# The tiles that TensorE reads in the feed-forward products at the lowest SBUF addresses: one core, local attention and a softplus feed-forward

## The chip, the core and the metric

The program runs on one core of a Trainium2 chip. The metric is the device time of one execution in microseconds (us), taken as the median of several runs. One execution was also recorded by the hardware profiler. Engines are named as in its page: PE is TensorE's matmul side, PEld its weight loads, DVE is VectorE, ACT ScalarE, POOL GpSimd, SP the engine that issues the DMAs.

## What is computed

Long-short attention (a window of 16 positions to each side, and one summary key and value for each block of 32), then a feed-forward network with softplus between its two products. Cut to what matters:

```python
k_sum = k.reshape(B, H, nb, 32, D).max(axis=3)      # B, H, S, D = 4, 8, 768, 64
v_sum = v.reshape(B, H, nb, 32, D).mean(axis=3)
scores_l = where(abs(i - j) < 16, q @ k.T / 8, -1e9)
scores_s = q @ k_sum.T / 8 + log(32)
a = softmax(concatenate([scores_l, scores_s], -1))
x = (a @ concatenate([v, v_sum], 2)).transpose(0, 2, 1, 3).reshape(3072, 512)
h = x @ w_in                                        # 512 -> 2048
g = maximum(h, 0) + log1p(exp(-abs(h)))             # softplus
out = g @ w_out                                     # 2048 -> 512
```

Everything comes in and leaves as float32.

## The kernel before

**Precision.** Both feed-forward products run in the type fp32r. Each operand is kept as two tiles or two halves of one, a rounded high part and the rest, and a product is made of three matmuls (high x high, high x rest, rest x high: `TERMS`).

**Tokens.** The 3072 tokens are worked on in six groups x = 0 to 5 of 512 (two chunks of 256). For each group the attention is done first (scores `sc`, L642, mask and maximum L655, exponential L663, division L676/L679, transposition, values `xo`, L740).

**Phases of the feed-forward.** `w_in` and `w_out` are cut into 16 pieces f of the hidden size; only 8 lie in SBUF at a time, in eight places of the pool `wts`. The phases run groups 0 to 4 over f = 0 to 7, then group 5 over all 16, then groups 4 down to 0 over f = 8 to 15. In the phases that begin at f = 0, `hidden` (L1058) makes one bank `ph` of 128x512 from 12 matmuls: the stationary operand is a piece of `w`, the moving one 512 columns of `xw`, the split input of the group. In the phases that begin at f = 8, `hidden_pair` (L1098) makes the two banks `hx` and `hy` of a pair of f by a Strassen-Winograd scheme with seven products of six 128x256 matmuls each; the moving operands are seven tiles `x` (operands 0 to 6), the stationary ones `w` or its sums `sw`.

**Second product.** ACT applies the softplus to the bank and writes the high part `gh` (L1160), then once more in place (L1164); DVE writes the rest `gl` (L1168). `feed_forward` (L1175) then adds 12 matmuls to four banks `po`: the stationary operand is a 128-column piece of `gh` (8 of the 12) or `gl` (4), the moving one 512 columns of `w`.

**Order.** What each engine does and in which order is written out by hand: `SEQUENCE` lists the tasks by number, `Order.issue` runs them in that order, and the semaphores between the engines follow from who writes and reads which tile. Nothing chooses an order by cost.

**Where tiles lie.** An SBUF tile has its address from its pool. Pools are laid out one after another in the order in which they are opened (`const`, `wts`, `work`), and within a pool each tag, with its number of buffers, gets its place when it first comes up. `wts` holds the weights `w` and, between them, the four places s0 to s3 of `sw` (and of the keys `kf` and values `st` that the attention sums up); `work` holds everything else, among it the inputs' places x0 to x6, `gh` and `gl`. `xw` of an odd group x uses the places x1 and x2 (two buffers each), `xw` of an even one the places x3 to x6.

Of the kernel before, what the change touches and what calls it, by code (L numbers as in the profile page):

```python
# [10 lines left out]
F32 = mybir.dt.float32  # L11
F32R = mybir.dt.float32r
# [220 lines left out]
def kernel(  # L233
# [11 lines left out]
    P = 128  # L245
    B, NHP, _, S = kT.shape
# [3 lines left out]
    NCC = DM // P  # L250
# [5 lines left out]
    CH = CHUNK  # L256
# [3 lines left out]
    CT = 2 * CH  # L260
# [5 lines left out]
    NU = 4  # L266
    NG = 2
# [4 lines left out]
    order = Order()  # L272
    const = ctx.enter_context(tc.tile_pool(name="const", bufs=1))
    wts = ctx.enter_context(tc.tile_pool(name="wts", bufs=1))
    work = ctx.enter_context(tc.tile_pool(name="work", bufs=2))
    dram = ctx.enter_context(tc.tile_pool(name="dram", bufs=3, space=bass.MemoryType.DRAM))
    psum = ctx.enter_context(tc.tile_pool(name="psum", bufs=2, space=bass.MemoryType.PSUM))

    def buffer(shape, dtype, name, tag=None, bufs=None, pool=work, dynamic=False):
        return Buffer(order, pool, shape, dtype, name, tag, bufs, dynamic)  # L280
# [48 lines left out]
        return buffer([P, 2 * WC], F32, name, tag=f, pool=wts, bufs=1)  # L329

    def sums_of(p, name):
        return buffer([P, 2, NU, CH], F32 if name == "first" else F32R, name, tag=f"s{p}", pool=wts, bufs=1)

    def operands(n, name):
        if n < 3:
            return buffer([P, 2, NG, CH], F32R, name, tag=f"x{n}", bufs=2)
        return buffer([P, 2, NG * CH], F32R, name, tag=f"x{n}", bufs=1)

    def block(n, name="r"):
        return buffer([P, NG * CH], F32, name, tag=f"r{n}")  # L340
# [2 lines left out]
    class Sums:  # L343
# [12 lines left out]
        def declare(self):  # L356
            order.group = f"s{self.b}"
            n_t = BLOCK // NHP
            rows = v_hp[self.b].rearrange("hp (n t) c -> (hp n) t c", t=BLOCK)
            self.kf = [buffer([P, 2, S], F32, "kf", tag=f"s{n}", pool=wts, bufs=1) for n in range(NHP // 2)]  # L360
            self.keys = lambda hp: self.kf[hp // 2]()[:, hp % 2]
            self.key_of = lambda hp: (self.kf[hp // 2], hp % 2)
            for i in range(NHP):
                st = buffer([P, n_t, P], F32, "st", tag=f"s{2 + i % 2}", pool=wts, bufs=1)

                def load_k(i=i):
                    nc.sync.dma_start(out=self.keys(i), in_=kT[self.b, i])
                order.add(SP, 0, load_k, [], [self.key_of(i)], size=384 * KiB, row=3072)

                def max_k(i=i):  # L370
                    self.max_keys(i, 0, self.keys(i))
                order.add(DVE, dve(S), max_k, [self.key_of(i)], [(self.k, i)])

                def load_v(i=i, st=st):
                    nc.sync.dma_start(out=st()[:NR], in_=rows[:, i * n_t:(i + 1) * n_t])
                order.add(SP, 0, load_v, [], [st], size=384 * KiB, row=4096)

                def sum_v(engine, st=st, i=i):
                    rows, v = st()[:NR], self.v()
                    for n in (4, 2):  # L380
                        engine.tensor_tensor(rows[:, :n], rows[:, :n], rows[:, n:2 * n], op=ALU.add)
                    if i:
                        engine.tensor_tensor(rows[:, 0], rows[:, 0], rows[:, 1], op=ALU.add)
                        engine.tensor_tensor(v, v, rows[:, 0], op=ALU.add)
                    else:
                        engine.tensor_tensor(v, rows[:, 0], rows[:, 1], op=ALU.add)
                order.add(
                    POOL, 3.0, lambda f=sum_v: f(nc.gpsimd), [st], [self.v],
                    ways=[Way(DVE, 1.8, lambda f=sum_v: f(nc.vector), port=True)],
                )  # L390

            def mean():
                nc.vector.tensor_scalar_mul(self.v(), self.v(), 1.0 / BLOCK)
            order.add(DVE, 0.22, mean, [], [self.v], port=True)
# [1 line left out]


        def declare_first(self):
            self.kf = [buffer([P, S], F32, "kf0", tag=f"x{1 - hp // 2}", bufs=2) for hp in range(NHP)]
            self.keys = lambda hp: self.kf[hp]()  # L400
            self.key_of = lambda hp: self.kf[hp]

            def load_k(hp):
                nc.sync.dma_start(out=self.keys(hp), in_=kT[self.b, hp])

            def max_k(hp):
                self.max_keys(hp, 0, self.keys(hp))
            for hp in range(NHP):
                order.add(SP, 0, lambda hp=hp: load_k(hp), [], [self.kf[hp]], size=384 * KiB, row=3072)
                order.add(DVE, dve(S), lambda hp=hp: max_k(hp), [self.kf[hp]], [(self.k, hp)])  # L410
# [39 lines left out]
    x_bufs = {}  # L450
# [148 lines left out]
    def whole_x(x):  # L599


        if x not in x_bufs and not x % 2:
            x_bufs[x] = [(buffer([P, 1, 2, CT], F32R, "xw", tag=f"x{3 + cc}", bufs=1), 0) for cc in range(NCC)]
        elif x not in x_bufs:
            x_bufs[x] = [(buffer([P, 1, 2, CT], F32R, "xw", tag=f"x{1 + cc % 2}", bufs=2), 0) for cc in range(NCC)]
        return x_bufs[x]

    def kept(x, n):
# [264 lines left out]
    def temporary(pair, outer, which, n):  # L873


        places = {
            (1, 0): ("x2", work, 2), (2, 0): ("x2", work, 2),
            (4, 0): ("q" if not which else "v", work, 1), (4, 1): ("k" if not which else "sp", work, 1),
            (5, 0): ("tb", work, 1), (5, 1): ("pT", work, 1), (6, 0): ("v", work, 1), (6, 1): ("sp", work, 1),
            (7, 0): ("tb", work, 1), (7, 1): ("pT", work, 1),  # L880
        }
        if (pair, outer) not in places:
            return buffer([P, n], U32, "t", "t", T_BUFS, dynamic=True)
        tag, pool, bufs = places[pair, outer]
        return buffer([P, n], U32, "t", tag, bufs, pool)
# [249 lines left out]
    def feed_forward(x, f0, f1):  # L1135
        po = [buffer([P, DM], F32, "po", "po", NT, psum) for _ in range(NT)]
        pairs = f0 > 0
        for f in range(f0, f1):
            if f0 == 0 and f == HALF:
                arrive(range(HALF, NF))  # L1140
            order.group = f"f{x}.{f}"
            if not pairs:
                hs, n = hidden(x, f), 0
            elif f % 2 == 0:
                hs, n = hidden_pair(x, f), 0
            else:
                n = 1
            order.group = f"f{x}.{f}"
            h = hs[n]
            halves = [(h, 0), (h, 1)] if pairs else [h]  # L1150
            w2, i2, _ = w_out_of[f]
            gh = buffer([P, CT], F32R, "gh", bufs=4)
            gl = buffer([P, CT], F32R, "gl", bufs=4)

            def all_of(h=h):
                return h().rearrange("p n c -> p (n c)") if pairs else h()


            def rounded(gh=gh, all_of=all_of):
                nc.scalar.activation(gh(), all_of(), AF.Softplus)  # L1160
            order.add(ACT, act(CT, True), rounded, halves, [gh], table="softplus")

            def exact(all_of=all_of):
                nc.scalar.activation(all_of(), all_of(), AF.Softplus)  # L1164
            order.add(ACT, act(CT, True), exact, [], halves, table="softplus")

            def rest(gh=gh, gl=gl, all_of=all_of):
                nc.vector.tensor_sub(out=gl(), in0=all_of(), in1=gh().bitcast(F32))  # L1168
            order.add(DVE, dve(CT), rest, [*halves, gh], [gl])

            def project(tokens, which, f=f, w2=w2, i2=i2, gh=gh, gl=gl):
                for t in tokens:
                    for i, (a, part) in enumerate(((gh, 0), (gh, 1), (gl, 0))):
                        if (a is gl) in which:
                            nc.tensor.matmul(  # L1175
                                po[t](), lhsT=a()[:, t * P:(t + 1) * P], rhs=w2()[:, part, i2 * DM:(i2 + 1) * DM],
                                start=f == f0 and i == 0, stop=f == f1 - 1 and i == 2,
                            )
            parts = [(w2, i) for i in range(2)]
            if f in (f0, f1 - 1):  # L1180
                for t in range(NT):
                    order.add(
                        PE, 0.7, lambda t=t, p=project: p([t], (False, True)), [gh, gl, *parts], [po[t]],
                    )
            else:
                every = range(NT)
                order.add(PE, 0.47 * NT, lambda p=project: p(every, (False,)), [gh, *parts], po)
                order.add(PE, 0.235 * NT, lambda p=project: p(every, (True,)), [gl, *parts], po)
# [45 lines left out]
    sums = Sums(0)  # L1234
# [67 lines left out]
    for x, f0, f1 in phases:  # L1302
        if x and not f0:
            sums = attend(x, sums)
# [43 lines left out]
```

## Time and profile before

| | us |
|---|---|
| median of 3 runs | 628.8 (627.85 to 631.18) |
| the profiled execution: its own time | 628.08 |
| the profiled execution: span from first to last instruction | 626.3 |
| PE busy in the span | 605.3 (97%) |
| PEld / DVE / ACT / POOL busy | 506.5 / 391.6 / 349.7 / 180.7 |

A matmul's end is modelled in the profile, and it is longer than the distance to the next one's start: consecutive matmuls overlap, and "busy" hides short stops. How fast PE goes is read from how many matmuls a stretch holds: the chain of the work that ended last counts them without overlap, and the timeline gives starts. The granted clock of TensorE is at its full level, 2.4 GHz, from 50 us after the start on.

### The profile page before, as it was taken

The page shows a single profiled execution, that of the slowest core. Times are in us where ns is not written, and L with a number is a line of the kernel's source. Part 1 is how long each engine was busy: PE and PEld are TensorE (multiplying, and loading weights), DVE is VectorE, ACT ScalarE, POOL GpSimd, SP SyncE. Part 2 cuts the span into 40 slices and gives each one's busy share as a digit, 9 for nine tenths or more (in the row PEclk, how much of TensorE's full clock was granted, in tenths as well). Part 3 has the DMA queues.
Part 4 walks back from the last instruction along what each step waited for, and adds up shares of the span by engine and source line. Part 5 has one row for each costly group of instructions (what it writes and reads, how often), then busy time and mean ns, then how long its engine had stood idle before and what let it go on. Part 6 is the DMA issues. An engine that isn't in the chain of part 4 may idle for free.

```text
span 626.3 us, 12000 instructions
## 1 busy us (share of the span) xinstructions
PE 605.3 (97%) x4452; PEld 506.5 (81%) x4452; DVE 391.6 (63%) x1010; ACT 349.7 (56%) x859; POOL 180.7 (29%) x180
## 2 busy tenths in 40 slices
PE   7668999999999999999999999999999999999997
PEld 6457777887787887888888888889888888989895
DVE  5989998686466755444316579873665664564532
ACT  4899999779667676665436886442312322132211
POOL 4444354041314222121000754474410325003000
PEclk9989999999999999999999999999999999999999
DMA  8986777977667676567435640023040230030031
GB/s 295 331 265 188 221 227 232 266 220 247 228 194 253 196 248 210 179 186 239 119 104 178 213 148 1 1 89 113 1 168 2 100 135 1 34 102 1 36 101 67
DMA packets 66570, 96.12 MB, mean 153 GB/s; under 512 B 5872, under 2 KB 44624, under 8 KB 65744
## 3 DMA queue, kind: packets, MB, share of 16 engines
q1 hardware_dynamic: 66512, 95.36, 48.0%
q8 instruction: 35, 0.57, 0.4%
q14 instruction: 23, 0.19, 0.1%
HBM read 66.06 MB, written 27.26 MB: 149 GB/s over the span
## 4 chain that ended last, share of the span: by engine, by line
PE 82%; DVE 6%; DMA 4%; SPq 3%; ACT 3%; issue 1%; ACTq 0%; DVEq 0%
PE po L1175 40%; PE ph L1058 20%; PE hx L1098 9%; PE hy L1098 7%; PE xo L740 3%; PE sc L642 2%; DMA squares<-tb 1%; DVE sp L655 1%; DMA kf<-kT_dram 1%; SPq L721 1%; SPq L513 1%; DVE w L972 1%; SPq L530 1%; ACT sp L679 1%; DVE ks L351 1%
## 5 line engine op out<-in xcount | busy, mean ns | idle before, releaser
L1175 PE MATMUL po<-w,gh 128*128 128x512 f32 x768 | 206.4, 397 | 0.0
L1175 PEld LDWEIGHTS po<-w,gh 128*128 128x128 f32 x768 | 141.6, 188 | 31.7 <-issue 0.6
L1058 PE MATMUL ph<-xw,w 128*128 128x512 f32 x672 | 163.1, 393 | 1.0 <-DVE xw L774 1.0
L1058 PEld LDWEIGHTS ph<-xw,w 128*128 128x128 f32 x672 | 125.7, 188 | 30.0 <-DVE xw L774 1.4
L1175 PE MATMUL po<-w,gl 128*128 128x512 f32 x384 | 116.1, 396 | 0.0
L1175 PEld LDWEIGHTS po<-w,gl 128*128 128x128 f32 x384 | 71.0, 188 | 15.9 <-issue 0.3
L663 ACT ACTIVATE sp<-sp,nm 128x120 f32<-128x120 f32 x192 | 73.1, 385 | 4.9 <-DVE nm L655 4.6
L1160 ACT ACTIVATE gh<-hx 128x512 fp32r<-128x512 f32 x20 | 12.0, 598 | 107.3 <-DVE hx L1108 107.3
L961 POOL TENSOR_TENSOR t<-t,raw 128x1024 int32<-128x1024 int32 (+1 forms) x20 | 41.9, 2100 | 95.8 <-DVE t L947 74.4
L1168 DVE TENSOR_TENSOR gl<-ph,gh 128x512 fp32r<-128x512 f32 x56 | 38.2, 686 | 45.1 <-ACT ph L1164 44.9
L1160 ACT ACTIVATE gh<-ph 128x512 fp32r<-128x512 f32 x56 | 33.4, 597 | 47.4 <-PE ph L1058 47.1
L802 POOL TENSOR_TENSOR x<-r,x 128x512 fp32r<-128x512 f32 x23 | 30.5, 1337 | 68.3 <-DVE x L795 58.6
L655 DVE CUSTOM_DVE_ANT_0 sp<-sc,added 128x120 f32<-128x120 f32 x192 | 40.9, 277 | 4.7 <-PE sc L642 3.9
L663 ACT ACTIVATION_READ_ACCUMULATOR sp<-sp,nm 128x1 f32 x192 | 36.4, 190 | 0.0
L1098 PE MATMUL hx<-x,w 128*128 128x256 f32 x240 | 35.6, 284 | 0.0
L1098 PE MATMUL hx<-x,sw 128*128 128x256 f32 x240 | 35.4, 283 | 0.0
L1098 PEld LDWEIGHTS hx<-x,w 128*128 128x128 f32 x240 | 32.7, 189 | 2.4
L1160 ACT ACT_TABLE_LOAD x23 | 29.5, 1283 | 8.9 <-PE ph L1058 8.6
L1098 PE MATMUL hy<-x,sw 128*128 128x256 f32 x240 | 34.1, 282 | 0.0
L1164 ACT ACTIVATE ph<-ph 128x512 f32<-128x512 f32 x56 | 33.0, 592 | 0.0
L1098 PEld LDWEIGHTS hx<-x,sw 128*128 128x128 f32 x240 | 31.8, 188 | 0.8
L709 DVE STREAM_TRANSPOSE tb<-sp 128x1024 f32<-128x1024 f32 x20 | 24.8, 1240 | 10.4 <-POOL sp L676 5.4
(113 smaller groups left out, 842.4 us busy)
## 6 DMA issues: line engine op xcount, KB each, us to landing
squares<-tb SPq DMA_DIRECT2D x20, 512.0 KB
pT<-squares SPq DMA_DIRECT2D x80, 128.0 KB
raw<-w_out_dram SPq DMA_DIRECT2D x16, 512.0 KB
kf<-kT_dram SPq DMA_DIRECT2D x16, 384.0 KB
raw<-w_in_dram SPq DMA_DIRECT2D x6, 1024.0 KB
q<-qT_dram SPq DMA_DIRECT2D x20, 256.0 KB
raw<-r SPq DMA_DIRECT2D x20, 256.0 KB
part<-ob SPq DMA_DIRECT2D x10, 512.0 KB
```

The lines of the kernel that those rows point to most:

```text
L655: nc.vector.tensor_tensor_reduce(out=sp()[:, n], in0=unit(n), in1=added()[:, kinds.index((lows[w], lows[w + 1]))], scale=-SCALE, scalar=FL ...
L663: nc.scalar.activation(sp()[:, n], sp()[:, n], AF.Exp, bias=nm()[:, n:n + 1], scale=-1.0, accum_out=ss()[:, n:n + 1],)
L709: nc.vector.transpose(out=tb().rearrange("p k (u q) -> p u k q", q=SQ), in_=tiles.sp().rearrange("p u (k q) -> p u k q", q=SQ),)
L740: nc.tensor.matmul(xo()[h * D:(h + 1) * D, g * CH + w * QW:g * CH + (w + 1) * QW], lhsT=tiles.v(g)[:, w, h * D:(h + 1) * D], rhs=queries(g ...
L802: engine.tensor_tensor(to(1), a(), to(0).bitcast(F32), op=ALU.subtract)
L961: nc.gpsimd.tensor_tensor(a, a, word(0, I32), op=ALU.add)
L1058: nc.tensor.matmul(ph(), lhsT=lhs(part, cc), rhs=xw[cc][0]()[:, xw[cc][1], a], start=cc == 0 and n == 0, stop=cc == NCC - 1 and n == 2,)
L1098: nc.tensor.matmul(to()[:, half], lhsT=lhs(wa, cc), rhs=of_x(xa)[:, cc * CH:(cc + 1) * CH], start=cc == 0 and m == 0, stop=cc == NG - 1 an ...
L1160: nc.scalar.activation(gh(), all_of(), AF.Softplus)
L1164: nc.scalar.activation(all_of(), all_of(), AF.Softplus)
L1168: nc.vector.tensor_sub(out=gl(), in0=all_of(), in1=gh().bitcast(F32))
L1175: nc.tensor.matmul(po[t](), lhsT=a()[:, t * P:(t + 1) * P], rhs=w2()[:, part, i2 * DM:(i2 + 1) * DM], start=f == f0 and i == 0, stop=f == ...
```

## The change

Two pools are opened between `wts` and `work`: `operands` and `sums`. Into `operands` go the tags x0 to x6 (and what else uses these places: the first group's keys and one kind of temporary), `gh` and `gl`. Into `sums` go s0 to s3. `wts` keeps only the weights. So the pools follow each other as constants, weights, operands, sums, the rest.

```diff
     wts = ctx.enter_context(tc.tile_pool(name="wts", bufs=1))
+    operand_pool = ctx.enter_context(tc.tile_pool(name="operands", bufs=1))
+    sums_pool = ctx.enter_context(tc.tile_pool(name="sums", bufs=1))
     work = ctx.enter_context(tc.tile_pool(name="work", bufs=2))
...
     def sums_of(p, name):
-        return buffer([P, 2, NU, CH], F32 if name == "first" else F32R, name, tag=f"s{p}", pool=wts, bufs=1)
+        return buffer([P, 2, NU, CH], F32 if name == "first" else F32R, name, tag=f"s{p}", pool=sums_pool, bufs=1)
...
         if n < 3:
-            return buffer([P, 2, NG, CH], F32R, name, tag=f"x{n}", bufs=2)
-        return buffer([P, 2, NG * CH], F32R, name, tag=f"x{n}", bufs=1)
+            return buffer([P, 2, NG, CH], F32R, name, tag=f"x{n}", bufs=2, pool=operand_pool)
+        return buffer([P, 2, NG * CH], F32R, name, tag=f"x{n}", bufs=1, pool=operand_pool)
...
-            self.kf = [buffer([P, 2, S], F32, "kf", tag=f"s{n}", pool=wts, bufs=1) for n in range(NHP // 2)]
+            self.kf = [buffer([P, 2, S], F32, "kf", tag=f"s{n}", pool=sums_pool, bufs=1) for n in range(NHP // 2)]
...
-                st = buffer([P, n_t, P], F32, "st", tag=f"s{2 + i % 2}", pool=wts, bufs=1)
+                st = buffer([P, n_t, P], F32, "st", tag=f"s{2 + i % 2}", pool=sums_pool, bufs=1)
...
-            self.kf = [buffer([P, S], F32, "kf0", tag=f"x{1 - hp // 2}", bufs=2) for hp in range(NHP)]
+            self.kf = [buffer([P, S], F32, "kf0", tag=f"x{1 - hp // 2}", bufs=2, pool=operand_pool) for hp in range(NHP)]
...
-            x_bufs[x] = [(buffer([P, 1, 2, CT], F32R, "xw", tag=f"x{3 + cc}", bufs=1), 0) for cc in range(NCC)]
+            x_bufs[x] = [(buffer([P, 1, 2, CT], F32R, "xw", tag=f"x{3 + cc}", bufs=1, pool=operand_pool), 0) for cc in range(NCC)]
         elif x not in x_bufs:
-            x_bufs[x] = [(buffer([P, 1, 2, CT], F32R, "xw", tag=f"x{1 + cc % 2}", bufs=2), 0) for cc in range(NCC)]
+            x_bufs[x] = [(buffer([P, 1, 2, CT], F32R, "xw", tag=f"x{1 + cc % 2}", bufs=2, pool=operand_pool), 0) for cc in range(NCC)]
...
-            (1, 0): ("x2", work, 2), (2, 0): ("x2", work, 2),
+            (1, 0): ("x2", operand_pool, 2), (2, 0): ("x2", operand_pool, 2),
...
-            gh = buffer([P, CT], F32R, "gh", bufs=4)
-            gl = buffer([P, CT], F32R, "gl", bufs=4)
+            gh = buffer([P, CT], F32R, "gh", bufs=4, pool=operand_pool)
+            gl = buffer([P, CT], F32R, "gl", bufs=4, pool=operand_pool)
```

In the built programs the instructions of every engine, their order and their waits are the same before and after; what differs are SBUF addresses, and PSUM's are the same. The addresses, in bytes from the start of each partition, are these (first byte of the lowest buffer to the end of the highest; the last column is the remainder of each buffer's start by 256):

| tiles | before | after | remainder before, after |
|---|---|---|---|
| weights `w` (eight places; before, s0 to s3 lie between them) | 18688 to 116992 | 18688 to 84224 | 0, 0 |
| `xw` of odd groups (places x1, x2) | 125184 to 145408 | 84224 to 100608 | 0, 0 |
| `x` operand 0 (place x0) | 158464 to 166656 | 100608 to 108800 | 0, 0 |
| `xw` of even groups, `x` operands 3 to 6 (places x3 to x6) | 182144 to 202624 | 108800 to 125184 | 128, 0 |
| `gh` | 202624 to 210816 | 125184 to 133376 | 128, 0 |
| `gl` | 210816 to 219008 | 133376 to 141568 | 128, 0 |
| `sw`, `kf`, `st` (places s0 to s3) | 35072 to 80128 | 141568 to 174336 | 0, 0 |
| keys `k` of the attention (moving operand of `sc`) | 133376 to 137216 | 182528 to 186368 | 0, 0 |
| queries `q` (stationary operand of `sc`) | 174976 to 177024 | 207744 to 209792 | 128, 128 |
| `pT`, `v` (operands of `xo`) | 177024 to 181120, 219008 to 223104 | 209792 to 213888, 219008 to 223104 | 128, 128 |

## Rows read from the trace of the kernel before

**Rows 1.** The page's busy times, then busy time by stretch, all engines, with granted clock.
```profile
PE 605.3 (97%) x4452; PEld 506.5 (81%) x4452; DVE 391.6 (63%) x1010; ACT 349.7 (56%) x859; POOL 180.7 (29%) x180
...
54.00:107.00 53.00, 51.58 (x465) 40.97 (x465) 47.66 (x133) 50.84 (x145) 21.60 (x16) 1.00 0.75 227
107.00:402.00 295.00, 294.99 (x2059) 238.34 (x2060) 177.55 (x480) 200.81 (x476) 75.75 (x78) 1.00 0.59 184
402.00:615.00 213.00, 213.00 (x1320) 190.74 (x1319) 118.58 (x239) 56.31 (x106) 57.83 (x46) 1.00 0.19 65
```

**Rows 2.** Waits of PE: line waited for, us in total, times, longest.
```profile
PE ph L1058 <- DVE xw L774: 1.0, 1, 1.0
...
PE xo L740 <- DVE gl L1168: 0.7, 1, 0.7
PE xo L740 <- DMA pT<-squares: 0.4, 1, 0.4
```

**Rows 3.** The chain that ended last, by engine, from the page.
```profile
PE 82%; DVE 6%; DMA 4%; SPq 3%; ACT 3%; issue 1%; ACTq 0%; DVEq 0%
```

**Rows 4.** Groups of PE by line and form: count, busy us, mean ns.
```profile
L1175 PE MATMUL po<-w,gh 128*128 128x512 f32 x768 | 206.4, 397 | 0.0
L1058 PE MATMUL ph<-xw,w 128*128 128x512 f32 x672 | 163.1, 393 | 1.0 <-DVE xw L774 1.0
L1175 PE MATMUL po<-w,gl 128*128 128x512 f32 x384 | 116.1, 396 | 0.0
...
L1098 PE MATMUL hx<-x,sw 128*128 128x256 f32 x240 | 35.4, 283 | 0.0
L1098 PE MATMUL hy<-x,sw 128*128 128x256 f32 x240 | 34.1, 282 | 0.0
...
L642 PE MATMUL sc<-k,q 64*64 64x120 f32 x640 | 21.0, 269 | 0.1
```

**Rows 5.** The chain's pieces on L1058: odd groups 1 and 5, even 2 and 4.
```profile
109.29 5.44 PE ph L1058 x24
...
172.94 4.20 PE ph L1058 x18
...
279.90 5.58 PE ph L1058 x24
...
326.87 5.45 PE ph L1058 x24
```

**Rows 6.** The chain's pieces on L1175: group 5's, and the last phase's.
```profile
395.22 7.44 PE po L1175 x32
...
608.60 12.55 PE po L1175 x54
```

**Rows 7.** Instructions of L1058 by stretch: groups 0, 2 and 4 (PE, PEld, clock).
```profile
54.00:107.00 53.00, 21.70 (x89) 16.60 (x89) 1.00 0.75 227
...
160.00:210.00 50.00, 23.86 (x96) 17.95 (x96) 1.00 0.73 230
...
268.00:319.00 51.00, 23.45 (x96) 18.05 (x96) 1.00 0.55 172
```

**Rows 8.** Timeline of PE in one pair of L1098: start, us, instructions.
```profile
570.74 0.88 PE L1098 MATMUL hx<-x,w 128*128 128x256 f32 x6
571.45 0.88 PE L1098 MATMUL hx<-x,sw 128*128 128x256 f32 x6
572.16 1.59 PE L1098 MATMUL hy<-x,sw 128*128 128x256 f32 x12
573.59 0.87 PE L1098 MATMUL hx<-x,sw 128*128 128x256 f32 x6
574.30 0.88 PE L1098 MATMUL hx<-x,w 128*128 128x256 f32 x6
```

**Rows 9.** The chain's longest pieces that are not PE's, inside 54 to 107 us.
```profile
80.62 5.52 DMA squares<-tb
...
91.63 2.65 DMA pT<-squares
```

## The prediction

> **What bounds the kernel now.** I looked first at the busy times by stretch [rows 1]. From 107 to 615 us PE has no idle time that they show (294.99 of 295.00 us, then 213.00 of 213.00), at the full clock; DVE has 178 of 295 and 119 of 213 us, ACT less in the second. The waits of PE say the same from the other side: after 54 us those of any length add up to about 2 us [rows 2]. The chain that ended last is 82% PE's [rows 3]. So from 54 us on the time is the number of PE's instructions times the distance from one's start to the next. The mean durations of the groups [rows 4] don't give that distance: 1152 matmuls of L1175 at 397 ns would be 457 us. It is read from the chain's pieces, where overlap is taken out.
>
> There the reader should see two speeds for the same instruction. L1058 is the same code in all six groups: 128x512, 12 matmuls into one bank, the same weights at the same addresses. In groups 1 and 5 a piece of 24 takes 5.44 and 5.45 us, 226.9 ns each; in groups 2 and 4 a piece of 18 takes 4.20 us and one of 24 takes 5.58, 233.3 and 232.5 ns each [rows 5]. They alternate with the group, from 109 to 332 us, so neither the clock nor how busy the neighbours are goes with them. What does differ is where `xw` lies: odd groups at 125184 to 145408, even ones at 182144 to 202624. L1175 runs at the slow speed in a phase of each kind: 32 matmuls in 7.44 us and 54 in 12.55, 232.5 and 232.4 ns [rows 6]. Its moving operand is always a weight at the low end, but its stationary one, `gh` or `gl`, lies at 202624 to 219008. The difference is 232.5 - 226.9 = 5.6 ns for a matmul of 512 columns.
>
> Of the cause the trace says only that it goes with the place. Two descriptions fit the address table: the slow operands lie high (from 182144 up), or they start 128 past a multiple of 256 while their partner starts on one. After the change `xw`, `gh` and `gl` lie at 84224 to 141568 and start on multiples of 256, so both descriptions put them at 226.9 ns.
>
> **The change, part by part.** No instruction, order or wait is added, removed or moved; only addresses are. So the terms are speeds.
>
> *`xw` of even groups (L1058).* Groups 0, 2 and 4 have 96 matmuls each [rows 7] (the stretch of group 0 cuts off a few). At 5.6 ns that is 288 x 5.6 = 1.6 us. The row for the new place is the odd groups', where 122 KiB to 142 KiB is fast as a moving operand; I take it whole.
>
> *`gh` and `gl` (L1175).* 768 + 384 = 1152 matmuls [rows 4], 1152 x 5.6 = 6.5 us. That a stationary operand costs by its place as a moving one does is an inference: no row has L1175 with a low `gh`. Between nothing and 6.5 us I take 6.5, because L1175 has the speed of the even groups to within 0.1 ns, and the other candidate, the writing to four banks in place of one, would have to cost the same by accident. After the change its two operands stand in the two regions in which odd groups' operands stand now, with the roles exchanged.
>
> *The 256-column products (L1098).* Five pieces of one pair start at 570.74, 571.45, 572.16, 573.59 and 574.30 us [rows 8]: 30 matmuls in 3.56 us, 0.71 us for every six. Operand 0 (at 158464), used by the first six, and operands from 182144 up, used by the next twelve, take the same 0.71. So moving `x` down is worth nothing here. `sw` goes up, from 35072 to 141568 and beyond, as a stationary operand; its new start is a multiple of 256. Bounds: nothing, as the moving operands show no effect in this shape, and 480 x 5.6 = 2.7 us if it costs as much as `gh` does now. I take nothing, the nearer row.
>
> *The attention's operands.* `k` goes from 133376 to 182528 as a moving operand of 640 matmuls on L642 [rows 4], `q`, `pT` and `v` were high and stay so. Nothing, or 640 x 5.6 = 3.6 us if each pays and none overlaps; it keeps its remainder by 256, and beside `q`, which is high already, I take nothing. DVE, ACT, POOL and DMA read and write at other addresses too; where one did get slower, rows 1 leave at least 80 us of DVE's time free in each of the two long stretches.
>
> *What the gain meets.* From 107 us on PE is never without work, so what it gains moves everything behind it forward. Between 54 and 107 us that isn't so: the chain goes through 5.52 us of the transposed squares' DMA and 2.65 of their return [rows 9], and a faster L1058 or L1175 arrives earlier at the same DMA. There lie the 96 matmuls of L1058 of group 0 and 96 of L1175: 192 x 5.6 = 1.1 us, which I don't count.
>
> Sum: 1.6 + 6.5 - 1.1 = 7.0 us. The profiled execution took 628.1 (span 626.3, 1.8 around it) and would take 621.1. It lies 0.7 under the median of 628.8, so the forecast for a median is 628.8 - 7.0 = 621.8 us. With the first stretch's 1.1 us, and some tenths from odd groups, whose first matmuls behind L1175 take longer too, 620.4; with a fifth of the gain met by waits that are short now, 623.2. Runs of before spread by 3.3 us, so I set 619 to 623.5 as this case's own range.
>
> **The rivals.**
>
> B: `gh`, `gl` and `xw` gain, and `sw` pays. 621.8 + 2.7 = 624.5. For it: `sw` becomes a stationary operand far from the weights' end, its last places beyond 145408, up to which operands at 226.9 ns are seen. Against it: L1098 takes no notice of where `x` lies.
>
> C: only a moving operand counts; L1175 is slow for a reason of its own, its change of banks. Then `xw` of groups 2 and 4 alone gains, 192 x 5.6 = 1.1 us: 627.7. For it: no row has another place of `gh`. Against it: the speeds are equal to 0.1 ns.
>
> D: the place counts for nothing, and odd and even groups differ by something that comes with them. Nothing moves: 628.8. Against it: L1058's code has no other difference by parity than its places. The Trainium skill speaks for D: by "SBUF — State Buffer", section "Who interferes with whom", PE has two read ports of its own and "PE and ACT never wait on anyone", with no word on addresses. The trace disagrees, with 226.9 against 232.5 ns on one line.
>
> E, the other side: height counts, and for a stationary operand it begins below 125184 (226.9 ns is seen with it up to 100608, 232.5 from 202624). Then `gh` and `gl` stay slow, `sw` becomes slow (+2.7), `k` as a moving operand above 182144 becomes slow too (+3.6), and only groups 2 and 4 gain (-1.1): 628.8 + 5.2 = 634.0. It decides from the point where a piece of six with `sw` goes from 0.71 us to 0.74. Against it: the remainder by 256 explains the same rows without any height, and `x` at 182144 and up costs nothing in L1098.
>
> **How the numbers follow.** My forecast A gets 0.72: the same line at two speeds is strong, the step to the stationary operand is the open one. B 0.09, C 0.09, D 0.05, E 0.05. A measurement here tells about 0.5% from no change, 3.1 us, so faster means under 625.7 and slower over 631.9. A and B are faster, 0.81; C and D within, 0.14; E slower, 0.05. The predicted time is A's, 621.8. A and B together hold 0.81, so the range is theirs with B's uncertainty of a us or two above: 619.0 to 626.0.
>
> **What would show it.** In the changed kernel's chain L1175 should have pieces of 24 in 5.45 us (12 in 2.72) where it has 5.58 (2.79) now, L1058 the same 5.45 in all groups; L1098 0.71 us for six with `w` and with `sw` alike; the stretch that begins with L1058 of group 1 and ends with the last L1175 shorter by about 7 us, and PE without idle time in it. Wrong would be: L1175 still at 232.5 (C, D or E), `sw` at 0.74 (B or E), or a PE that is faster and then waits, for DVE's combinations in L1098's phases above all.

## The result

The changed kernel takes 623.1 us (median of 6 runs, 622.96 to 625.77), the kernel before 628.8 (6 runs beside it, 627.85 to 631.18): a ratio of 0.991, interval 0.989 to 0.994. The profiled execution took 623.92 us with a span of 622.1, against 628.08 and 626.3.

The page of the changed kernel, busy times and shares of the chain that ended last, against [rows 1] and [rows 3]: PE has the same 4452 instructions and 6.1 us less of busy time, and the other engines keep theirs within 2 us.

```profile
PE 599.2 (96%) x4452; PEld 506.4 (81%) x4452; DVE 389.8 (63%) x1010; ACT 349.6 (56%) x859; POOL 180.7 (29%) x180
...
PE 83%; DVE 7%; ACT 4%; DMA 2%; SPq 2%; issue 1%; ACTq 0%; DVEq 0%
```

The lines of the code have moved by two: L1060 is the first product (`ph`), L1177 the second (`po`), L1100 the pairs. The chain's pieces on L1060 and L1177 (start in us, length, count), two of group 1, one each of groups 2, 4 and 5 and two of the second product, answer to [rows 5] and [rows 6]:

```profile
109.25 5.44 PE ph L1060 x24
131.71 5.67 PE ph L1060 x24
...
173.19 4.10 PE ph L1060 x18
...
278.66 5.44 PE ph L1060 x24
...
309.15 6.80 PE po L1177 x30
324.74 5.44 PE ph L1060 x24
...
604.75 12.28 PE po L1177 x54
```

Group 4's piece of 24, 5.58 us before at 279.90, is now 5.44 like those of groups 1 and 5, and group 2's piece of 18, 4.20 before, is 4.10; the last 54 matmuls of the second product take 12.28 us in place of 12.55, 227.4 ns each, and 30 in a row 226.7. The difference between the kinds of group is gone. (Group 1's piece of 5.67 us begins behind the attention's matmuls: its first distance is 336 ns and the next six are 228 to 236; only then come 227. Group 3's of this kind took 5.70 in the kernel before.)

### The profile page after: what moved, and what is told of

The parts are those of the page before. It is cut to its first block, busy times and chain, and to the rows that moved or that the text cites. A ratio compares the mean times of both kernels' runs of the same rounds, so it can differ in the third digit from the quotient of the medians.

```text
span 622.1 us, 12000 instructions
## 1 busy us (share of the span) xinstructions
PE 599.2 (96%) x4452; PEld 506.4 (81%) x4452; DVE 389.8 (63%) x1010; ACT 349.6 (56%) x859; POOL 180.7 (29%) x180
## 4 chain that ended last, share of the span: by engine, by line
PE 83%; DVE 7%; ACT 4%; DMA 2%; SPq 2%; issue 1%; ACTq 0%; DVEq 0%
PE po L1177 38%; PE ph L1060 21%; PE hx L1100 9%; PE hy L1100 7%; PE xo L742 4%; PE sc L644 3%; DVE sp L657 1%; DMA raw<-w_out_dram 1%; DVE t L941 1%; DVE w L974 1%; ACT t L937 1%; ACT sp L681 1%; DVE ks L353 1%; DMA v<-vs 1%; SPq L723 1%
## 5 line engine op out<-in xcount | busy, mean ns | idle before, releaser
L1177 PE MATMUL po<-w,gh 128*128 128x512 f32 x768 | 203.2, 392 | 0.1
L1177 PEld LDWEIGHTS po<-w,gh 128*128 128x128 f32 x768 | 141.1, 188 | 29.7 <-DVE ob L1207 0.7
L1060 PE MATMUL ph<-xw,w 128*128 128x512 f32 x672 | 161.2, 391 | 1.0 <-DVE xw L776 1.0
L1060 PEld LDWEIGHTS ph<-xw,w 128*128 128x128 f32 x672 | 125.6, 188 | 28.2 <-DVE xw L776 1.4
L1177 PE MATMUL po<-w,gl 128*128 128x512 f32 x384 | 114.3, 391 | 0.0
L1177 PEld LDWEIGHTS po<-w,gl 128*128 128x128 f32 x384 | 70.9, 188 | 14.4 <-issue 0.3
L1100 PE MATMUL hx<-x,w 128*128 128x256 f32 x240 | 35.7, 285 | 0.0
L1100 PE MATMUL hx<-x,sw 128*128 128x256 f32 x240 | 35.5, 284 | 0.0
L1100 PEld LDWEIGHTS hx<-x,w 128*128 128x128 f32 x240 | 32.9, 190 | 2.1
L1100 PE MATMUL hy<-x,sw 128*128 128x256 f32 x240 | 34.4, 284 | 0.0
L1100 PEld LDWEIGHTS hx<-x,sw 128*128 128x128 f32 x240 | 32.0, 190 | 0.8
L1100 PEld LDWEIGHTS hy<-x,sw 128*128 128x128 f32 x240 | 31.2, 191 | 0.2
```

What stands on the lines that cost most here:

```text
L1060: nc.tensor.matmul(ph(), lhsT=lhs(part, cc), rhs=xw[cc][0]()[:, xw[cc][1], a], start=cc == 0 and n == 0, stop=cc == NCC - 1 and n == 2,)
L1100: nc.tensor.matmul(to()[:, half], lhsT=lhs(wa, cc), rhs=of_x(xa)[:, cc * CH:(cc + 1) * CH], start=cc == 0 and m == 0, stop=cc == NG - 1 an ...
L1177: nc.tensor.matmul(po[t](), lhsT=a()[:, t * P:(t + 1) * P], rhs=w2()[:, part, i2 * DM:(i2 + 1) * DM], start=f == f0 and i == 0, stop=f == ...
```

## Where the time went

I matched every matmul of one trace with the same one of the other and added up the distances from each start to the next. Up to 107 us the sum is the same within 0.3 us, as forecast. From there to 402 us the changed kernel is 2.9 us shorter, and from 402 us to the end 1.2; its two repeats below give 3.0 and 1.2 both times. So the traces show a gain of 4.2 us (4.5 in the repeats), where the sum of the prediction said 7.0. By instruction, in the first of these traces:

| from 107 us on | matmuls | forecast, us | measured, us |
|---|---|---|---|
| first product | 576 | -1.1 | -1.5 (-1.2 and -1.1 in the repeats) |
| second product to 402 us, without its one wait | 554 | -3.1 | -2.9 |
| that wait, on DVE, and the slow start behind it | | 0 | +0.4 (0.8 in each repeat) |
| second product from 402 us | 509 | -2.8 | -1.6 |
| pairs (L1100) | 840 | 0 | +0.4 |
| attention | 928 | 0 | +1.1 (0.2 and 0.3 in the repeats) |

Three of these rows say something.

**Short pieces gained nothing.** From 402 us on the second product comes in pieces between the 256-column matmuls of the pairs. First the chain's pieces of the kernel before, rows that no earlier section showed:

```profile
439.49 6.50 PE po L1175 x28
...
480.83 0.93 PE po L1175 x4
483.42 4.63 PE po L1175 x20
...
508.58 0.70 PE po L1175 x3
...
525.47 5.58 PE po L1175 x24
...
544.06 1.38 PE po L1175 x6
```

The same pieces of the changed kernel:

```profile
436.43 6.37 PE po L1177 x28
...
477.45 0.93 PE po L1177 x4
480.02 4.56 PE po L1177 x20
...
505.14 0.70 PE po L1177 x3
...
521.93 5.47 PE po L1177 x24
...
540.38 1.39 PE po L1177 x6
```

Pieces of 28, 24 and 20 are 0.13, 0.11 and 0.07 us shorter; those of 6, 4 and 3 aren't shorter at all, and 4 in 0.93 us is 232.5 ns each with the new addresses too. Start by start, the first five matmuls of 512 columns after a stretch of 256-column ones most often take 233, 236, 228, 233 and 231 ns, and only then 226.7. There are 41 such changes from 402 us on, and 183 of the 509 matmuls are among the first five behind one: together they take 0.2 us more than before, where the forecast had 1.0 less. That is the shortfall of that row, 1.2 us; the other 326 gain 1.8 us, 5.7 ns each. (Up to 402 us the first five behind the attention's matmuls gain nothing either, but there are only 89 of them in both products.)

**The pairs pay a little.** The timeline of PE in the changed kernel (start, us, instructions) through the pair of [rows 8]:

```profile
567.01 0.88 PE L1100 MATMUL hx<-x,w 128*128 128x256 f32 x6
...
568.44 1.60 PE L1100 MATMUL hy<-x,sw 128*128 128x256 f32 x12
569.88 0.88 PE L1100 MATMUL hx<-x,sw 128*128 128x256 f32 x6
570.60 0.88 PE L1100 MATMUL hx<-x,w 128*128 128x256 f32 x6
```

30 matmuls from 567.01 to 570.60 make 3.59 us where it was 3.56, 0.72 for every six where `x` is one of operands 3 to 6. It is the places of those operands that do it, not those of `sw`: e2 below moves operands 3 to 6 and leaves `sw` where it was, and there L1103, the same line, pays 0.4 us too; e6, which moves neither, leaves the line unchanged (+0.06).

**The gain meets DVE once.** At the end of the stretch up to 402 us PE now comes 3 us earlier to weights that DVE is still combining. The timeline of PE in the second repeat, the waits of PE in the first, and the chain of the changed kernel there (columns as before; the timeline's bracket is idle time and what ended it):

```profile
394.79 1.88 PE L1177 MATMUL po<-w,gh 128*128 128x512 f32 x7 [0.47 <-DVE w L974]
```

```profile
PE po L1177 <- DVE w L974: 0.5, 1, 0.5
```

```profile
388.48 3.05 DVE sw L1031
391.53 0.60 DVE x L804
392.13 1.21 DVE ws L1000 x2
393.34 0.60 DVE x L804
393.94 1.15 DVE w L974
```

This is the wait that the prediction named as a thing to look for, though at 395 us and not in the pairs' phases. The attention's +1.1 in this trace is mostly one wait of a values' matmul on a transfer (here of 1.0 us, 0.3 in one repeat, absent in the other):

```profile
PE xo L742 <- DMA st<-v_hp_dram: 1.0, 1, 1.0
```

The traces' 4.2 us and the medians' 5.6 agree within what the runs can tell: the interval of the ratio is 4.0 to 7.0 us, this trace of before lies 0.7 below its median and that of after 0.8 above. On the chips of the repeats the medians' gain is 5.7 and 5.4 us. All figures by instruction rest on the one trace of before, a run faster than its median, so about 1 us of the medians' gain is not placed by them.

## Experiments

The prediction left two descriptions of the slow place open, its height and the remainder of its start by 256, and rested on the step from the moving operand to the stationary one. All kernels below compute everything; only addresses differ, by unused tiles of some bytes per partition. In the tables of remainders the moving operand stands first, and distances are means over matmuls with neighbours of their own kind, after 107 us. Line numbers differ a little from kernel to kernel; `ph` is the first product, `po` the second, `hx` and `hy` are the pairs everywhere.

**e1: low, but 128 past a multiple of 256.** The changed kernel, all its operands 128 bytes further on; the sums above them back on multiples of 256.

```diff
     wts = ctx.enter_context(tc.tile_pool(name="wts", bufs=1))
+    gap_a = ctx.enter_context(tc.tile_pool(name="gap_a", bufs=1))
+    gap_a.tile([P, 32], F32, name="gap_a", tag="gap_a")
     operand_pool = ctx.enter_context(tc.tile_pool(name="operands", bufs=1))
+    gap_b = ctx.enter_context(tc.tile_pool(name="gap_b", bufs=1))
+    gap_b.tile([P, 32], F32, name="gap_b", tag="gap_b")
     sums_pool = ctx.enter_context(tc.tile_pool(name="sums", bufs=1))
```

> The changed kernel with a gap of 128 bytes in front of the operands' pool and another in front of the sums' pool: `x`, `xw`, `gh` and `gl` lie low (84352 to 141696), but start 128 past a multiple of 256; weights and sums keep the remainder 0. Theory H (height decides): L1177 and L1060 as in the changed kernel, 226.7 ns from start to start, 24 in 5.45 us, about 623 us. Theory R (the remainder by 256 decides): L1177 and the L1060 of all six groups at 232.5 ns, 24 in 5.58 us, and as the odd groups lose too, 628.8 + 384 x 5.6 ns = 631 us, at least 628.8.

Measured: 630.5 us, 1.002 [1.000, 1.003] of before, and 6.5 us over the changed kernel on the same chip (624.0, run a1). The chain's pieces, the first in an odd group, the next two in groups 4 and 5:

```profile
108.99 5.59 PE ph L1064 x24
...
281.03 5.58 PE ph L1064 x24
...
328.14 5.60 PE ph L1064 x24
...
611.13 12.55 PE po L1181 x54
```

All groups are slow, the odd ones too, and the second product has before's 12.55. The operands lie low here; 128 bytes take the whole gain away.

**e2: high, but on multiples of 256.** The kernel before, with 128 bytes ahead of the place x3, so that x3 to x6, `gh` and `gl` stay high.

```diff
         self.tile = None
+        self.gap = None
+        if tag == "x3" and (pool.name, tag) not in order.rings:
+            self.gap = lambda: pool.tile([128, 32], F32, name="gap", tag="gap", bufs=1)
...
         if self.tile is None:
+            if self.gap:
+                self.gap()
             self.tile = self.make()
```

> The kernel before with a gap of 128 bytes in front of the place x3: `xw` of even groups, `gh` and `gl` stay high (182272 to 219136) but start on multiples of 256, as `tb` and `v` do then. Theory H: nothing moves, L1175 and the even groups' L1058 at 232.5 ns, 628.8 us. Theory R: both at 226.7 ns, 24 in 5.45 us, about 623 us.

Measured: 624.9 us, 0.992 [0.989, 0.994]. The chain's pieces:

```profile
279.25 5.44 PE ph L1063 x24
...
605.77 12.28 PE po L1180 x54
```

Fast, with the operands above 182144. Height is out; 128 bytes in the kernel before do what the change does. It also bounds the remainder from above: the operands start at 182272, a multiple of 512, the weights at 18688, 256 past one, so a difference of 256 bytes costs nothing.

**e3: everything 128 past.** As e1, with the gap ahead of the weights, so that weights and operands agree.

```diff
+    gap_a = ctx.enter_context(tc.tile_pool(name="gap_a", bufs=1))
+    gap_a.tile([P, 32], F32, name="gap_a", tag="gap_a")
     wts = ctx.enter_context(tc.tile_pool(name="wts", bufs=1))
     operand_pool = ctx.enter_context(tc.tile_pool(name="operands", bufs=1))
+    gap_b = ctx.enter_context(tc.tile_pool(name="gap_b", bufs=1))
+    gap_b.tile([P, 32], F32, name="gap_b", tag="gap_b")
     sums_pool = ctx.enter_context(tc.tile_pool(name="sums", bufs=1))
```

> The changed kernel with the gap of 128 bytes in front of the weights: weights, `x`, `xw`, `gh` and `gl` all start 128 past a multiple of 256, low; the sums keep the remainder 0. Theory H: 226.7 ns, 623 us. Theory R in the form that both operands must agree: 226.7 ns for L1177 and L1060, 623 us, since weights and inputs have the same remainder. Theory R in the form that each operand must start on a multiple of 256: 232.5 ns everywhere, 631 us or more.

Measured: 625.6 us, 0.993 [0.990, 0.995]. The chain's pieces:

```profile
278.62 5.44 PE ph L1064 x24
...
604.53 12.28 PE po L1181 x54
```

So it isn't the multiple of 256 that is fast but the agreement: both operands at the same remainder, 0 or 128.

**a1 and a2: the changed kernel again**, beside e1 to e3 and beside b2 and b3.

> The changed kernel beside the others on their chip. Both theories: 226.7 ns on L1177 and L1060, 0.991 of the kernel before, about 623 us.

> The changed kernel beside b2_pairs_32 on its chip: 0.991 of the kernel before, 226.7 ns settled on L1177 and L1060, 120 on L1100.

Measured: 624.0 and 623.6 us, 0.991 [0.988, 0.995] and 0.992 [0.990, 0.993]; their traces are read above.

**e4 and e5: 64 and 32 bytes.** As e1 with another distance; one run each. The diff is against e1:

```diff
-    gap_a.tile([P, 32], F32, name="gap_a", tag="gap_a")
+    gap_a.tile([P, 16], F32, name="gap_a", tag="gap_a")
...
-    gap_b.tile([P, 32], F32, name="gap_b", tag="gap_b")
+    gap_b.tile([P, 48], F32, name="gap_b", tag="gap_b")
```

(e5 has 8 and 56 in these places.)

> The changed kernel with `x`, `xw`, `gh` and `gl` shifted by 64 bytes against the weights, all else with the remainders of the changed kernel. Theory R256 (the two operands of a matmul must agree in their remainder by 256, whatever the difference): 232.5 ns on L1177 and L1060, 24 in 5.58 us, about 630 us in the mean of runs as with 128. Theory R128 (only the bit of 128 counts, halves of 256 bytes): with 64 both starts are in the same half, 226.7 ns or a speed between, 623 to 627 us.

> The same with 32 bytes. Theory R256: 232.5 ns, about 630 us. Theory R128, or one in which the cost grows with the distance: 226.7 to 229 ns, 623 to 626 us.

Measured: 629.7 and 631.1 us, beside 629.0 of before. The chain's pieces of e4, then those of e5:

```profile
281.20 5.51 PE ph L1064 x24
...
344.07 5.60 PE po L1181 x24
...
610.20 12.60 PE po L1181 x54
```

```profile
282.32 5.60 PE ph L1064 x24
...
611.52 12.62 PE po L1181 x54
```

A difference of 32 or 64 costs as much as one of 128 (with 64 the first product somewhat less, 230.4 ns against 232.5). Any of the distances tried is slow. One run of a kernel says little of its time; the reading rests on the distances, and theory R128 falls with them, though for 64 in the first product it had named a speed between.

**e6: `gh` and `gl` alone.** The kernel before with the 128 bytes ahead of `gh`; `xw` of even groups keeps its remainder of 128. The diff is against e2:

```diff
-        if tag == "x3" and (pool.name, tag) not in order.rings:
+        if (tag or name) == "gh" and (pool.name, tag or name) not in order.rings:
```

> The kernel before with `gh` and `gl` alone (and `v`) moved up by 128 bytes, to a multiple of 256; `xw` of even groups keeps its remainder of 128. Theory R with operands that must agree: L1178 has 226.7 ns, even groups' L1061 keeps 232.5, odd ones 226.7; the gain is the part of L1178, about 4.5 of the 5.6 us, 624 to 625 us. Theory C of the prediction (only the moving operand counts): nothing moves, 628.8 us or a little under 630 on the chip of the first runs.

Measured: 624.3 us, 0.993 [0.992, 0.994]. The chain's pieces, group 4, group 5 and the second product:

```profile
279.14 5.57 PE ph L1063 x24
...
325.70 5.44 PE ph L1063 x24
...
605.60 12.29 PE po L1180 x54
```

The stationary operand alone brings nearly the whole gain, and even groups stay slow in the first product. In total e6 can't be told from e2: what `xw` brings, 1.1 to 1.6 us by the count, is within their intervals.

**b1: the attention's `q`.** The changed kernel with 128 bytes ahead of `q`, so that both operands of the scores start on multiples of 256. The diff is against e6, on the changed kernel:

```diff
-        if (tag or name) == "gh" and (pool.name, tag or name) not in order.rings:
+        if (tag or name) == "q" and (pool.name, tag or name) not in order.rings:
```

> The changed kernel with `q` and what lies above it moved up by 128 bytes, so that the attention's scores too have operands of one remainder (`k` 0, `q` 0; `pT` and `v` agreed before and do after). Theory R for every shape: L644's 640 matmuls gain up to 5.6 ns each where they don't overlap, 0 to 3.6 us under the changed kernel, of which the stretch from 107 us on may show 1 to 2 us. Theory R for 512 columns alone, as L1100 with its 256 suggests: nothing, 0.991 of the kernel before as the changed kernel.

Measured: 624.1 us, 0.992 [0.991, 0.994], no better than the changed kernel. The scores' group in b1, then in the changed kernel (count, busy us, mean ns):

```profile
L649 PE MATMUL sc<-k,q 64*64 64x120 f32 x640 | 21.3, 271 | 0.7 <-DVE nm L662 0.5
```

```profile
L644 PE MATMUL sc<-k,q 64*64 64x120 f32 x640 | 21.0, 269 | 0.3
```

For these matmuls of 120 columns and 64 rows the agreement does nothing: the distance is 26.05 ns in the mean in both.

**b2 and b3: the pairs out of step.** e4 and e5 had shown the 256-column matmuls slightly faster with unequal remainders. The timeline of PE in e5, against the one of the changed kernel above:

```profile
573.89 0.86 PE L1104 MATMUL hx<-x,w 128*128 128x256 f32 x6
574.59 0.86 PE L1104 MATMUL hx<-x,sw 128*128 128x256 f32 x6
575.29 1.56 PE L1104 MATMUL hy<-x,sw 128*128 128x256 f32 x12
576.69 0.86 PE L1104 MATMUL hx<-x,sw 128*128 128x256 f32 x6
577.39 0.86 PE L1104 MATMUL hx<-x,w 128*128 128x256 f32 x6
```

0.70 for six, 3.50 for the 30. So b2 sets the sums 32 bytes on, and operands 0, 1 and 6, which meet `w`, 32 bytes into their tiles; the second product stays in agreement. b3 does the same with 224 bytes.

```diff
+    gap_a = ctx.enter_context(tc.tile_pool(name="gap_a", bufs=1))
+    gap_a.tile([P, 8], F32, name="gap_a", tag="gap_a")
     sums_pool = ctx.enter_context(tc.tile_pool(name="sums", bufs=1))
...
     def operands(n, name):
+        if n in (0, 1, 6):
+            return buffer([P, 2 * NG * CH + 64], F32R, name, tag=f"x{n}", bufs=2 if n < 3 else 1, pool=operand_pool)
...
         def to(part):
+            if n in (0, 1, 6):
+                return buf()[:, 8 + part * NG * CH:8 + (part + 1) * NG * CH]
```

(In b3, 56 takes the place of both 8s. A second gap behind the sums, not shown, fills each up to 256 bytes.)

> The changed kernel, in which the 512-column products keep operands of one remainder by 256 and the 256-column ones get operands 32 apart: the pool of the sums begins 32 bytes later (`sw` at remainder 32, met by `x` operands 2 to 5 at 0), and the `x` operands 0, 1 and 6, which meet the weights at 0, lie 32 bytes inside tiles of 256 bytes more. From the rows of e5_low_32, where L1104's 256 columns took 116.8 ns in the mean against 119.5 in the changed kernel: theory F (the difference of remainders alone, in either role, speeds up 256 columns) 840 x 2.7 = 2.3 us at most, about 1.7 as e5's stretch showed, so 1.5 to 2.3 us under the changed kernel. Theory G (it was something of e5's own, or holds for the moving operand alone): 360 x 2.7 = 1.0 us or nothing.

> The same as b2_pairs_32 with 224 bytes, that is 32 the other way round. If the size of the difference decides, as b2_pairs_32: 117 ns on the 256 columns, 1.5 to 2.3 us under the changed kernel. If its sign does: 119 to 120 ns and no gain, 0.991 of the kernel before.

Measured: 624.0 us, 0.992 [0.990, 0.993], and 623.6, 0.992 [0.989, 0.994], the same as a2. The chain's pieces of the pairs in b2, then in the changed kernel:

```profile
567.13 1.42 PE hy L1108 x12
568.55 1.41 PE hx L1108 x12
```

```profile
568.61 1.44 PE hy L1100 x12
570.05 1.44 PE hx L1100 x12
```

The effect is there, 0.02 to 0.03 us for twelve. The pairs gain 1.1 us in b2 and 1.0 in b3 against the changed kernel; the stretch from 402 us is shorter by 0.8 and 1.3 us, and the total doesn't show it. Theory F's 1.5 to 2.3 us was not reached, and G had the size but not the reason, since both roles gain. The sign counts: in b2 the products with `w`, whose moving operand is 32 ahead of the stationary one, take 117.0 ns and those with `sw`, where it is 32 behind, 118.2; in b3, with the signs exchanged, they take 118.5 and 116.9. Both expectations had overlooked that each kernel holds both signs.

## Why the prediction held

**The reading of two speeds was right.** The cause was the addresses, and 226.9 and 232.5 ns were its two values. The two candidates for the place fell into one by e1 to e3: height does nothing, the remainder does, and more exactly whether it is the same for both operands. The prediction's own wording, "128 past a multiple of 256 while their partner starts on one", holds; e3 shows that the second half of it is the half that counts.

**The step to the stationary operand was right.** It was the open one. e6 moves `gh` and `gl` only, and the second product goes from 12.55 us for 54 to 12.29.

**The term of 6.5 us for L1175 was mis-sized.** It took the distance of long pieces for all 1152 matmuls. Of the 1063 behind 107 us those before 402 us gained 2.9 of 3.1 us, less 0.4 to 0.8 for a new wait; those behind it 1.6 of 2.8, since at each change from 256 to 512 columns five matmuls run at the old distance whatever the addresses. Taking the pieces by length would not have settled it: in the chain of before the pieces of 4 had 0.93 us, 232.5 ns each, and those of 3 and 6 had 230 to 233, the same as long ones. What a short piece would take with agreeing operands that trace couldn't tell, since it has none behind 256 columns; but a range for it was due, from nothing to 5.6 ns for each matmul of this stretch, 2.8 us. The medians' gain of 5.6 us comes nearer to the 7.0 of the sum than the traces' 4.2 to 4.5, but no term of the sum is the reason: about 1 us of it stands in no trace, and that the forecast of 621.8 came within 1.3 us of the median is in part luck.

**L1098 at nothing was nearly right**, +0.4 where nothing was forecast. "So moving `x` down is worth nothing here" rested on 0.71 us for six, two digits; and one ns in 840 matmuls is 0.8 us. The starts give one digit more, 118.7 ns for operand 0 and 118.5 for the others; the changed kernel's 119.5 was not to be seen in either.

**The 1.1 us of the first stretch** were rightly left out: there the sum of distances is unchanged within 0.3 us, and the attention waits for its transfers as before.

**The rivals.** B asked for `sw` at a higher price than `w`; both have 0.71 to 0.72 us for six. C (a moving operand alone counts) falls with e6, D (the place counts for nothing) with e1, which differs from the changed kernel by 128 bytes and by 6.5 us. On D the Trainium skill, "SBUF — State Buffer", section "Who interferes with whom", has PE reading through ports of its own that wait for nobody. That rule is about waiting for other engines, and the two speeds don't contradict it as the prediction said: no run here shows PE waiting for another engine's port; what e1 shows is that PE's own distance between matmuls changes with its addresses, 226.7 to 232.7 ns. E (height) falls with e2, whose operands lie above 182144 and take 5.44 us for 24.

## What to carry to other kernels

Give the two operands of a long run of 512-column matmuls the same remainder by 256: one unused tile of 128 bytes per partition ahead of them was worth as much here (e2, e6) as the new layout, within what the runs can tell. To find such an effect, look for one line of code with two speeds and compare starts, in pieces of the chain of equal length. Before multiplying a difference by a count, take the count of those instructions that run in pieces long enough to show it, and look at what the next engine is doing where PE will arrive earlier.

## What the runs showed of the hardware

| columns | remainders by 256, moving and stationary | ns from start to start |
|---|---|---|
| 512 | 0, 0 | 227.0 to 228.1 (226.7 in long pieces) |
| 512 | 128, 128 | 227.2 to 227.8 |
| 512 | 128, 0 and 0, 128 | 232.3 to 232.8 |
| 512 | 64, 0 and 0, 64 | 230.4 and 233.3 |
| 512 | 32, 0 and 0, 32 | 233.3 both |
| 256 | 0, 0 and 128, 128 | 118.7 to 119.7 and 119.3 |
| 256 | 128, 0 | 118.5 to 119.1 |
| 256 | 64, 0; 32, 0; 0, 32; 224, 0; 0, 224 | 117.7; 116.8 to 117.0; 118.2; 118.5; 116.9 |

I had expected none of three things: that only the agreement counts, that matmuls of 256 columns go slightly faster with remainders 32 or 64 apart, and that a run of 512-column matmuls needs five of them (27 ns in all) to reach its speed behind 256-column ones, while one that follows another 512-column product needs none. For 256 columns the remainders of the two operands aren't all that counts: e6 leaves operand 0 and the weights where they were in the kernel before, and yet operand 0's matmuls go from 118.5 to 119.7 ns there (those between two of their own). Why the agreement matters isn't settled by these runs: nothing in the traces separates the reading of the moving operand from the loading of the next weights beside it. Besides 256 (e2, e6), other differences than 32, 64 and 128 bytes weren't tried with 512 columns, nor was any of this with a matmul that needs no new weights.
